# Two transformer layers on one core: the first block's V product cut finer, its weights loaded in quarters, and its k products and attention moved later

## The chip, the cores and the metric

The kernel runs on one core of a Trainium2 chip. The metric is the device time of one execution in microseconds (us), lower being better. Most executions of one kernel agree within about 0.1%, which here is 1 to 2 us. In the profiles, PE is TensorE, DVE is VectorE, ACT is ScalarE and POOL is GpSimd.

## The reference

The input x has 2048 rows of 1024 numbers in bfloat16. An attention layer A and a gated layer B are applied, and then both once more with the same weights:

```python
def A(x):                        # on layernorm(x); H = 32 heads of 32, W = 8 keys, every 2nd position back
    q, k, v = split_heads(x @ wqkv)
    kg, vg  = k[idx], v[idx]     # idx = pos - {0, 2, ..., 14}, masked below 0
    attn    = softmax(einsum("bhsd,bhswd->bhsw", q, kg) * scale)
    return merge_heads(einsum("bhsw,bhswd->bhsd", attn, vg)) @ wo

def B(x):                        # on layernorm(x); F = 3584
    gate = x @ W_gate
    return ((gate * (gate > 0)) * (x @ W_up)) @ W_down

x = x + A(layernorm(x)); x = x + B(layernorm(x))
x = x + A(layernorm(x)); x = x + B(layernorm(x))
```

## The kernel before

The rows are handled in four blocks of 512, each of four tiles of 128 rows. TensorE does all products. VectorE does the attention of a block (products of q and k, sums, weighted sums of v) while TensorE is busy with other products, and between its attention steps it multiplies gate and up (`hT`). The program is a list of steps with planned times; the steps are emitted in the order of these times, and each engine runs its own in that order. `GRP` (1.73 us) is the planned time of one group of eight 512-column products. DMA transfers are mostly issued by the sync engine (SP), one after another in the order of the program.

At the start of the program nothing can be multiplied until the first tile is loaded, normalised and turned (transposed), and the first V weights are there. Before the change, V starts on two tiles, and its weights come in two loads of 1 MB (a slab is one such load), each with all of the contraction for half of the columns:

```python
    load_x(0)                                    # the four tiles of block 0, then the weights
    ...
    def want_v(key, mid, end):                   # two slabs of 512 columns, 1 MB each
        for g in range(2):
            want((key, g), wqkv_v[:, :, 2 * D + g * SLAB:2 * D + (g + 1) * SLAB], mid if g == 0 else end)
    ...
        scratch(14)                              # ln_first: 14 products that only keep TensorE busy
        bn(0, 0); bn(0, 1); aggr(0)              # (statements joined here)
        bn(1, 0); bn(1, 1); aggr(1)
        st1 = act_stats(2)
        apply(0); turn(0); apply(1)
        copy(0, "a", 1); copy(0, "a", 0)
        turn(1)
        act_vpe(2, st1)
        copy(1, "v", 0); copy(1, "a", 1)
        bn(3, 0); bn(3, 1); apply(2); aggr(3); apply(3)
        hold["later"] = {2: (lambda: (turn(2), ...)), 4: (lambda: (turn(3), ...))}
    ...
    def v_first(ln):                             # tiles 0-1, then 2-3, then all four at once
        plan = [(c, 0, 2) for c in range(6)] + [(c, 2, 4) for c in range(6)] + [(c, 0, 4) for c in range(6, KC)]
```

The order of q and k of block 0, and the place of its attention, which the change also moves:

```python
    QK_FIRST = [(nm, c) for c in range(KC) for nm in ("q", "k")]     # q0 k0 q1 k1 ...
    QK_ORDER = [("q", 0), ("q", 1)]                                  # q0 q1, then q2 k0 q3 k1 ...
    ...
        order = QK_FIRST if n < NB else QK_ORDER
    ...
    spread(prod_sum_steps(0), t_qk0 + 3.5, 4.4)
    ev.append((t_v2 + 3.2 * GRP, lambda: head_mm(0)))                # the head sum, L
    spread(softmax_steps(0), t_v2 + 3.3 * GRP, 0.01)
    t_pv0 = t_v2 + 2.2 * GRP + 10.0
```

And the gate and up products with their accumulators. A pool of six PSUM banks serves these accumulators:

```python
    psum = ctx.enter_context(tc.tile_pool(name="psum", bufs=6, space=bass.MemoryType.PSUM))
    ...
                for nm in ("g", "u"):                                # pair j of 28
                    acc = psum.tile([P, BLK], F32, tag="acc", name=f"acc_{nm}")
                    ... # eight products into acc
                    if nm == "g":
                        ... nc.scalar.activation(rs[j][:], acc[:], ACT.Relu)      # frees the gate bank early
                    else:
                        ups[j] = acc
        def gate(j):                                                 # frees the up bank, when VectorE gets to it
                dv(nc.vector.tensor_tensor, hold["hT"][:, j, :], ups.pop(j)[:], rs.pop(j)[:], op=ALU.mult)
```

## Time and profile before

| | before |
|---|---|
| time, median of 3 runs | 1619.39 us (1618.84 to 1619.86) |
| span of the profiled execution | 1617.51 us |
| scratch products end, tile 0 turned from | 6.70, 7.36 us |
| first V product, first q product | 9.83, 24.67 us |
| first V weights landed (two loads) | 9.79, 12.79 us |
| head sum of block 0's attention | 100.74 us |

The page's first part (busy time, share of the span, instructions, per engine) and the first line of its chain of work that ended last say that the kernel is bound by TensorE (PE) from end to end:

```profile
PE 1608.1 (99%) x7505; PEld 784.1 (48%) x7554; DVE 1138.3 (70%) x963; ACT 475.8 (29%) x971; POOL 176.1 (11%) x164
...
PE 99%; DMA 0%; issue 0%; SPq 0%; DVE 0%; DVEq 0%
```

The view of waits of PE (engine, line, for what: us in total, times, longest) has four entries, all within the first 10 us:

```profile
PE scratch L132 <- DVE ones L290: 1.5, 1, 1.5
PE acc_v L132 <- DMA w_v<-in_A_wqkv_dram: 0.9, 1, 0.9
PE tp L358 <- DVE xn_first L106: 0.7, 1, 0.7
PE tp L358 <- DVE mean L106: 0.4, 1, 0.4
```

PE's timeline there (start and duration in us, then what was done, and in brackets the idle time before it with what ended it) shows where a change can gain:

```profile
6.11 0.59 PE L132 MATMUL scratch<-ones 128*128 128x512 bf16 x2
7.36 0.62 PE L358 MATMUL tp<-ident,xn_first 128*128 128x128 bf16 x8 [0.66 <-DVE xn_first L106]
8.35 0.62 PE L358 MATMUL tp<-ident,xn_first 128*128 128x128 bf16 x8 [0.37 <-DVE mean L106]
9.83 1.38 PE L132 MATMUL acc_v<-xnT_first,w_v 128*128 128x256 bf16 x11 [0.86 <-DMA w_v<-in_A_wqkv_dram]
```

Two tiles are turned before the first product, and the last thing that the first product waits for is its weights. After this PE has nothing to wait for: a microsecond gained here is worth a microsecond at the end, unless something later takes it back.

A second place: the gate and up stage of block 0, near 230 us. The timeline of all engines there (SPq is the sync engine's issue of a DMA):

```profile
228.89 1.88 DVE L106 TENSOR_TENSOR hT<-acc_u,r 128x512 bf16<-128x512 f32 x3
229.00 0.34 SPq L121 DMA_DIRECT2D s_d<-s  x1
229.07 1.89 PE L132 MATMUL acc_g<-xnT_b,w_g 128*128 128x512 bf16 x8
230.80 1.46 PE L132 MATMUL acc_u<-xnT_b,w_u 128*128 128x512 bf16 x6
```

VectorE has fallen behind and does three `hT` products in a row; the first of these, for pair 8, ends at 229.57. The up product of pair 11 starts at 230.80.

### The profile page before, as it was taken

Reading aid. Unit: us, or ns where it says so; the run is one execution under the profiler, and the core shown is the slowest. Engines: PE = TensorE matmul, PEld = TensorE weight load, DVE = VectorE, ACT = ScalarE, POOL = GpSimd, SP = SyncE. Lnnn points to the kernel's source line nnn. Section 1 sums busy time; section 2 is a strip of 40 time slices with the busy share of each in tenths; the row PEclk is TensorE's granted clock in tenths of the full one; section 3 lists DMA queues with packets and bytes.
Section 4 is the critical chain, followed back from the end, with each engine's and each line's share of the span. In section 5 each row is a group of like instructions: output and inputs, shape, how many; then the busy total and the mean of one; then the engine's idle time right before and its main releaser. Section 6 shows DMA issues by size and latency. Waiting matters only on the chain.

```text
span 1617.5 us, 18722 instructions
## 1 busy us (share of the span) xinstructions
PE 1608.1 (99%) x7505; PEld 784.1 (48%) x7554; DVE 1138.3 (70%) x963; ACT 475.8 (29%) x971; POOL 176.1 (11%) x164
## 2 busy tenths in 40 slices
PE   9999999999999999999999999999999999999999
PEld 6646544444444445444454444544445444444444
DVE  6999979996989698929489293893939939311211
ACT  4853311131116313603136031361313311131110
POOL 2300100010003002300053000530005100000000
PEclk9999999999999999999999999999999999999999
DMA  9868867697669767794747948479574884755452
GB/s 295 184 197 251 213 173 244 182 213 206 209 189 216 202 183 216 188 248 144 229 160 202 240 152 230 153 203 254 160 231 155 207 240 156 209 171 167 155 169 66
DMA packets 408440, 317.92 MB, mean 197 GB/s; under 512 B 166432, under 2 KB 389024, under 8 KB 407840
## 3 DMA queue, kind: packets, MB, share of 16 engines
q1 hardware_dynamic: 407776, 316.13, 69.4%
q8 instruction: 59, 0.97, 0.2%
q10 hardware_dynamic: 576, 0.59, 0.1%
q14 instruction: 29, 0.24, 0.1%
HBM read 266.29 MB, written 34.66 MB: 186 GB/s over the span
## 4 chain that ended last, share of the span: by engine, by line
PE 99%; DMA 0%; issue 0%; SPq 0%; DVE 0%; DVEq 0%
PE acc_u L132 24%; PE acc_g L132 24%; PE dacc L132 18%; PE acc_v L132 7%; PE acc_q L132 7%; PE acc_k L132 7%; PE acc_wo L132 7%; PE dacc_pair L132 6%; DMA w_v<-in_A_wqkv_dram 0%; PE tp L358 0%; SPq L121 0%; PE L L132 0%; DVE x L778 0%; SPq L118 0%; DVEq L1017 0%
## 5 line engine op out<-in xcount | busy, mean ns | idle before, releaser
L132 PE MATMUL acc_g<-xnT_b,w_g 128*128 128x512 bf16 x1792 | 423.3, 379 | 0.0
L132 PE MATMUL acc_u<-xnT_b,w_u 128*128 128x512 bf16 x1792 | 423.3, 379 | 0.0
L731 ACT ACTIVATE r<-acc_g 128x512 bf16<-128x512 f32 x224 | 133.6, 596 | 728.7 <-PE acc_g L132 703.8
L106 DVE TENSOR_TENSOR hT<-acc_u,r 128x512 bf16<-128x512 f32 x224 | 151.0, 687 | 243.3 <-PE acc_u L132 240.8
L132 PE MATMUL dacc<-w_d,hT 128*128 128x512 bf16 (+1 forms) x1372 | 300.4, 375 | 1.5
L132 PEld LDWEIGHTS <-hT 128*128 128x128 bf16 x1820 | 178.1, 98 | 209.0
L132 PEld LDWEIGHTS <-w_g 128*128 128x128 bf16 x1792 | 175.4, 98 | 211.4
L132 PEld LDWEIGHTS <-w_u 128*128 128x128 bf16 x1792 | 175.3, 98 | 211.4
L106 DVE TENSOR_TENSOR pv<-a,vhm 128x4096 bf16<-128x4096 bf16 x64 | 143.6, 2285 | 0.0
L778 DVE TENSOR_TENSOR x<-dacc,x 128x512 bf16<-128x512 f32 (+1 forms) x38 | 24.5, 673 | 154.1 <-PE dacc L132 154.1
L549 DVE TENSOR_TENSOR t<-q,k 128x2048 f32<-128x2048 bf16 x56 | 128.0, 2292 | 6.7 <-ACT k L485 4.6
L106 DVE TENSOR_TENSOR t<-q,k 128x2048 f32<-128x2048 bf16 x56 | 127.5, 2287 | 3.9 <-ACT k L485 2.4
L106 DVE TENSOR_TENSOR pv<-pv 128x1024 bf16<-128x1024 bf16 (+1 forms) x128 | 113.8, 952 | 0.0
L132 PE MATMUL acc_wo<-w_o,oT 128*128 128x512 bf16 x498 | 111.1, 379 | 0.7
L249 POOL TENSOR_TENSOR st_b<-st_b,neg_half 128x1 f32<-128x1 f32 x29 | 43.8, 1517 | 609.9 <-ACT st_b L248 609.9
L562 DVE TENSOR_TENSOR ac<-ac,t 128x2048 f32<-128x2048 f32 x48 | 109.7, 2285 | 0.3
L106 DVE TENSOR_TENSOR ac<-ac,t 128x2048 f32<-128x2048 f32 x48 | 109.7, 2285 | 0.0
L490 POOL COPY kh<-k 128x14 bf16<-128x14 bf16 x40 | 53.7, 1348 | 506.5 <-ACT k L485 410.4
L132 PE MATMUL dacc_pair<-w_d,hT 128*128 128x512 bf16 x413 | 95.5, 379 | 0.4
L132 PEld LDWEIGHTS <-oT 128*128 128x128 bf16 x512 | 50.1, 98 | 60.4
L244 ACT ACTIVATE xn_b<-x 128x1024 bf16<-128x1024 bf16 x29 | 30.3, 1047 | 128.6 <-DVE x L106 66.5
L410 ACT CAST vT<-acc_v 128x512 bf16<-128x512 f32 x56 | 32.7, 586 | 54.0 <-PE acc_v L132 54.0
(131 smaller groups left out, 1226.8 us busy)
## 6 DMA issues: line engine op xcount, KB each, us to landing
w_g<-in_B_W_gate_dram SPq DMA_DIRECT2D x56, 1024.0 KB, 7.2
w_u<-in_B_W_up_dram SPq DMA_DIRECT2D x56, 1024.0 KB, 5.5
w_d<-in_B_W_down_dram SPq DMA_DIRECT2D x48, 1024.0 KB, 6.0
w_o<-in_A_wo_dram SPq DMA_DIRECT2D x16, 1024.0 KB, 6.6
vhm<-v_d SPq DMA_DIRECT2D x32, 284.0 KB, 6.7
v_d<-vT SPq DMA_DIRECT2D x8, 1024.0 KB, 9.0
oT<-o_d SPq DMA_DIRECT2D x32, 256.0 KB, 4.5
w_d<-in_B_W_down_dram SPq DMA_DIRECT2D x16, 512.0 KB, 3.7
```

The source lines that it names most:

```text
L106: tail_dve[0] = f(*args, **kwargs).ins
L132: tail_pe[0] = nc.tensor.matmul(*args, **kwargs).ins
L244: nc.scalar.activation(xn, xt[:], ACT.Square, accum_out=sq)
L249: nc.gpsimd.tensor_tensor(rstd, vpe, neg_half[:, 0:1], op=ALU.pow)
L410: tail_act[0] = nc.scalar.copy(st["vT"][:, c, :], acc[:]).ins
L490: nc.gpsimd.tensor_copy(khalo[n][:, c, :], k[:, BLK:BLK + HALO])
L549: nc.vector.tensor_tensor(t[:], i0, i1, op=ALU.mult)
L562: nc.vector.tensor_tensor(o, ac[:], t[:], op=ALU.add)
L731: tail_act[0] = nc.scalar.activation(rs[j][:], acc[:], ACT.Relu).ins
L778: run = dv if n < NB - 2 else (lambda f, *args, **kwargs: f(*args, **kwargs))
```

## The change

The intent is to let PE begin V as soon as one tile is turned and a quarter of V's weights is in. V's weights are cut by the contraction instead of by columns, and each half comes in two transfers of 512 KB. V is first computed for tile 0 alone, over the first half of the contraction; tile 1, 2 and 3 follow as they become ready, and the second half is added later. The turns of tiles 1, 2 and 3 stand between V products (before, only those of tiles 2 and 3 did). A few small steps move from VectorE to ScalarE and GpSimd (POOL), x's fourth tile is loaded after the first weights, and the k products of block 0 start two PE groups later, with its attention.

```diff
-    load_x(0)
+    load_x(0, range(TPB - 1))
...
+    def want_v_first(end0, end1):
+        for hh, end in enumerate((end0, end1)):
+            want(("v0", hh), qkv_half(2, hh), end)
...
+    def load_slab(key, src):
...
+        if key[0] == "v0":
+            for i in range(2):
+                rows = slice(i * (KC // 4), (i + 1) * (KC // 4))
+                sp_dma(tv[:, rows, :], src[:, rows, :])
...
+    load_slab(("v0", 0), qkv_half(2, 0))
+    load_x(0, [TPB - 1])
+    load_slab(("v0", 1), qkv_half(2, 1))
+    load_slab(("qk01", "q", 0), qkv_half(0, 0))
...
-        scratch(14)
+        scratch(13)
         bn(0, 0); bn(0, 1); aggr(0)
+        act_square(2); act_mean(2)
         bn(1, 0)
+        apply(0, 0); apply(0, 1)
+        turn(0)
+        copy(0, "a", 0)
         bn(1, 1); aggr(1)
+        copy(0, "v", 1)
+        act_power(2)
+        apply(1, 0); apply(1, 1)
+        def second():
+            turn(1)
+            apply(2)
+            copy(1, "v", 0); copy(1, "v", 1)
+            act_square(3); act_mean(3); act_power(3)
+            apply(3)
...
-        plan = [(c, 0, 2) for c in range(6)] + [(c, 2, 4) for c in range(6)] + [(c, 0, 4) for c in range(6, KC)]
+        def head():                              # tile 0, first half of the contraction
+            for kc in range(KC // 2):
+                if kc == KC // 2 - 1:
+                    ln["second"]()
+                for c in range(KC):
+                    prod(kc, c, 0, 1)
+        ...                                      # then tiles 1, 2, 3; then the second half, two tiles at a time
...
-        order = QK_FIRST if n < NB else QK_ORDER
+        order = QK_STAGED if staged else QK_ORDER          # QK_STAGED is QK_FIRST renamed; block 0 is not staged
...
-    spread(prod_sum_steps(0), t_qk0 + 3.5, 4.4)
+    spread(prod_sum_steps(0), t_qk0 + GRP * K_STEP[0] + 1.8, 4.4)
-    ev.append((t_v2 + 3.2 * GRP, lambda: head_mm(0)))
-    spread(softmax_steps(0), t_v2 + 3.3 * GRP, 0.01)
-    t_pv0 = t_v2 + 2.2 * GRP + 10.0
+    ev.append((t_v2 + 5.2 * GRP, lambda: head_mm(0)))
+    spread(softmax_steps(0), t_v2 + 5.3 * GRP, 0.01)
+    t_pv0 = t_v2 + 4.2 * GRP + 10.0
```

Statements are joined with semicolons here, and removed helper lines are left out.

More of the change, by code (lines that the diff above doesn't have):

```diff
@@ L169, with load_x @@
         x_tiles.append(xt)
-    def load_x(b):
-        for t in range(b * TPB, (b + 1) * TPB):
+    def load_x(b, tiles=range(TPB)):
+        for t in (b * TPB + i for i in tiles):
             if t == 0:
@@ L192, in want_v, with qkv_half @@
             want((key, g), wqkv_v[:, :, 2 * D + g * SLAB:2 * D + (g + 1) * SLAB], mid if g == 0 else end)
+    def qkv_half(i, hh):
+        return wqkv_v[:, hh * (KC // 2):(hh + 1) * (KC // 2), i * D:(i + 1) * D]
+    def want_v_first(end0, end1):
+        for hh, end in enumerate((end0, end1)):
+            want(("v0", hh), qkv_half(2, hh), end)
     def want_qk(key, q_end, k_end):
@@ L196, in want_qk @@
             for hh in range(2):
-                want((key, nm, hh), wqkv_v[:, hh * (KC // 2):(hh + 1) * (KC // 2), i * D:(i + 1) * D], end)
+                want((key, nm, hh), qkv_half(i, hh), end)
     def want_wo(n, mid, end):
@@ L213, in want_down @@
             want(("d", n, half, s), wd_v[:, rows, half * SLAB:(half + 1) * SLAB], at + gap * min(8 * (s + 1), FC))
+    def load_slab(key, src):
+        shp = list(src.shape)
+        t = wring.tile([P, 8 * SLAB], BF16, tag="slab", name="w_" + "_".join(str(k) for k in key))
+        tv = t[:, 0:shp[1] * shp[2]].rearrange("p (a b) -> p a b", b=shp[2])
+        if key[0] == "v0":
+            for i in range(2):
+                rows = slice(i * (KC // 4), (i + 1) * (KC // 4))
+                sp_dma(tv[:, rows, :], src[:, rows, :])
+        else:
+            sp_dma(tv, src)
+        slab[key] = tv
     def slab_events(events):
         for i, (key, src, _) in enumerate(slab_plan):
-            def f(key=key, src=src):
-                shp = list(src.shape)
-                t = wring.tile([P, 8 * SLAB], BF16, tag="slab", name="w_" + "_".join(str(k) for k in key))
-                tv = t[:, 0:shp[1] * shp[2]].rearrange("p (a b) -> p a b", b=shp[2])
-                sp_dma(tv, src)
-                slab[key] = tv
+            if key in slab:
+                continue
             ends = sorted(end for _, _, end in slab_plan[:i])
-            events.append((ends[i - RING] + 0.3 if i >= RING else 0.1 * i, f))
+            events.append((ends[i - RING] + 0.3 if i >= RING else 0.1 * i, lambda key=key, src=src: load_slab(key, src)))
     def ln_steps(n, which, early=False, dve=()):
@@ L313, in small @@
             return stat_pool.tile([P, 1], F32, tag="f" + name, name=name, bufs=bufs)
-        mean, vpe, rstd, bst = {}, {}, {}, {}
+        mean, rstd, bst, sq = {}, {}, {}, {}
         def bn(t, half):
@@ L324, in aggr @@
             on("v", nc.vector.bn_aggr, mv[:], bst[t][:].rearrange("p a b -> p (a b)"))
-            vpe[t], mean[t] = small("vpe1"), mv[:, 0:1]
-            on("v", nc.vector.tensor_scalar, vpe[t][:], mv[:, 1:2], EPS, None, op0=ALU.add)
-            power(t)
-        def power(t):
-            rstd[t] = small("rstd1")
-            on("g", nc.gpsimd.tensor_tensor, rstd[t][:], vpe[t][:], neg_half[:, 0:1], op=ALU.pow)
-        def act_stats(t):
-            st1 = stat_pool.tile([P, 2], F32, tag="st1", name="st1")
-            on("a", nc.scalar.activation, xna[:, t, :], x_tiles[t][:], ACT.Identity, accum_out=st1[:, 0:1])
-            on("a", nc.scalar.activation, xna[:, t, :], x_tiles[t][:], ACT.Square, accum_out=st1[:, 1:2])
-            return st1
@@ L339, in act_vpe, with power, act_square @@
-        def act_vpe(t, st1):
+            mean[t] = mv[:, 0:1]
+            power(t, mv[:, 1:2], 1.0)
+        def power(t, var, sign):
+            rstd[t], vpe = small("rstd1"), small("vpe1")
+            on("g", nc.gpsimd.tensor_scalar, vpe[:], var, sign, EPS, op0=ALU.mult, op1=ALU.add)
+            on("g", nc.gpsimd.tensor_tensor, rstd[t][:], vpe[:], neg_half[:, 0:1], op=ALU.pow)
+        def act_square(t):
+            sq[t] = small("sq1")
+            on("a", nc.scalar.activation, xna[:, t, :], x_tiles[t][:], ACT.Square, scale=float(D) ** -0.5,
+               accum_out=sq[t][:])
@@ L340, in act_vpe, with act_mean, act_power @@
+        def act_mean(t):
             mn = small("mean1")
-            on("v", nc.vector.tensor_scalar, mn[:], st1[:, 0:1], 1.0 / D, None, op0=ALU.mult)
+            on("a", nc.scalar.activation, xna[:, t, :], x_tiles[t][:], ACT.Identity, scale=1.0 / D, accum_out=mn[:])
+            mean[t] = mn[:]
+        def act_power(t):
             nvar = small("nvar1")
-            on("v", nc.vector.scalar_tensor_tensor, nvar[:], st1[:, 0:1], mn[:], st1[:, 1:2], op0=ALU.mult, op1=ALU.subtract)
-            vpe[t], mean[t] = small("vpe1"), mn[:]
@@ L345, in act_vpe, with apply @@
-            on("v", nc.vector.tensor_scalar, vpe[t][:], nvar[:], -1.0 / D, EPS, op0=ALU.mult, op1=ALU.add)
-            power(t)
-        def apply(t):
-            on("v", nc.vector.tensor_scalar, xna[:, t, :], x_tiles[t][:], mean[t], rstd[t][:],
+            on("v", nc.vector.scalar_tensor_tensor, nvar[:], mean[t], mean[t], sq[t][:], op0=ALU.mult, op1=ALU.subtract)
+            power(t, nvar[:], -1.0)
+        def apply(t, half=None):
+            cols = slice(0, D) if half is None else slice(half * SLAB, (half + 1) * SLAB)
+            on("v", nc.vector.tensor_scalar, xna[:, t, cols], x_tiles[t][:, cols], mean[t], rstd[t][:],
@@ L354, in turn @@
         def turn(t):
-            tps[t] = [psum.tile([P, KC // 2, P], BF16, tag="acc", name=f"tp{h}") for h in range(2)]
+            if t == 0:
+                tps[t] = [psum.tile([P, KC // 2, P], BF16, tag="acc", name=f"tp{h}")[:] for h in range(2)]
+            else:
+                both = psum_l.tile([P, 2, KC, P], BF16, tag="L", name="tp_pair")
+                tps[t] = [both[:, h, 0:KC // 2, :] for h in range(2)]
             for c in range(KC):
@@ L362, in copy @@
             f = nc.vector.tensor_copy if eng == "v" else nc.scalar.copy
-            on(eng, f, hold["xnT"][:, t, h * (KC // 2):(h + 1) * (KC // 2), :], tps[t][h][:])
+            on(eng, f, hold["xnT"][:, t, h * (KC // 2):(h + 1) * (KC // 2), :], tps[t][h])
         warm = small("warm")
         on("a", nc.scalar.activation, warm[:], ones[:, 0:1], ACT.Identity)
-        scratch(14)
+        scratch(13)
         bn(0, 0)
@@ L370, in ln_first @@
         aggr(0)
+        act_square(2)
+        act_mean(2)
         bn(1, 0)
+        apply(0, 0)
+        apply(0, 1)
+        turn(0)
+        copy(0, "a", 0)
         bn(1, 1)
         aggr(1)
-        st1 = act_stats(2)
-        apply(0)
-        turn(0)
-        apply(1)
-        copy(0, "a", 1)
-        copy(0, "a", 0)
-        turn(1)
-        act_vpe(2, st1)
-        copy(1, "v", 0)
-        copy(1, "a", 1)
-        bn(3, 0)
-        bn(3, 1)
-        apply(2)
-        aggr(3)
-        apply(3)
-        hold["later"] = {2: (lambda: (turn(2), copy(2, "a", 0), copy(2, "v", 1))),
-                         4: (lambda: (turn(3), copy(3, "v", 0), copy(3, "a", 1)))}
+        copy(0, "v", 1)
+        act_power(2)
+        apply(1, 0)
+        apply(1, 1)
+        def second():
+            turn(1)
+            apply(2)
+            copy(1, "v", 0)
+            copy(1, "v", 1)
+            act_square(3)
+            act_mean(3)
+            act_power(3)
+            apply(3)
+        hold["second"], hold["last"] = second, last
+        hold["later"] = {t: (lambda t=t: (turn(t), copy(t, "a", 0), copy(t, "v", 1))) for t in (2, 3)}
         return hold
@@ L416, in v_first @@
         st = att[0]
-        plan = [(c, 0, 2) for c in range(6)] + [(c, 2, 4) for c in range(6)] + [(c, 0, 4) for c in range(6, KC)]
-        def f_(i, c, t0, t1):
-            def f():
-                if i == 0:
-                    st["vT"] = big_tile([P, KC, BLK], "vT_0", True)
-                acc = psum.tile([P, BLK], F32, tag="acc", name="acc_v")
-                cols = slice(t0 * P, t1 * P)
-                with pe_group():
-                    for kc in range(KC):
-                        mm(acc[:, cols], lhsT=slab[("v0", c // 4)][:, kc, (c % 4) * P:(c % 4 + 1) * P],
-                           rhs=ln["xnT"][:, t0:t1, kc, :], start=(kc == 0), stop=(kc == KC - 1))
-                tail_act[0] = nc.scalar.copy(st["vT"][:, c, cols], acc[:, cols]).ins
-                if i in ln["later"]:
-                    ln["later"][i]()
-            return f
@@ L434, in v_first, with prod @@
-        at, out = 0.0, []
-        for i, (c, t0, t1) in enumerate(plan):
-            out.append((at, f_(i, c, t0, t1)))
-            at += GRP * (t1 - t0) / TPB
-        return out
+        pairs, opened = {}, set()
+        def prod(kc, c, t0, t1):
+            part = t0 // 2
+            if (part, c // 2) not in pairs:
+                pairs[part, c // 2] = psum.tile([P, 2, BLK // 2], F32, tag="acc", name="acc_v")
+            acc = pairs[part, c // 2][:, c % 2, (t0 % 2) * P:(t0 % 2 + t1 - t0) * P]
+            with pe_group():
+                mm(acc, lhsT=slab["v0", kc // (KC // 2)][:, kc % (KC // 2), c * P:(c + 1) * P],
+                   rhs=ln["xnT"][:, t0:t1, kc, :], start=(part, c // 2) not in opened, stop=(kc == KC - 1),
+                   skip_group_check=True)
+            opened.add((part, c // 2))
@@ new lines, in head, with first_half @@
+        def head():
+            st["vT"] = big_tile([P, KC, BLK], "vT_0", True)
+            for kc in range(KC // 2):
[3 more added lines that the diff above has]
+                    prod(kc, c, 0, 1)
+        def first_half(t):
+            def f():
+                for c in range(KC):
+                    if t == 2 and c == KC // 2:
+                        ln["later"][3]()
+                    for kc in range(KC // 2):
+                        prod(kc, c, t, t + 1)
+            return f
@@ new lines, in second_half, with f @@
+        def second_half(i, t0):
+            def f():
+                if (i, t0) == (2, 0):
+                    ln["later"][2]()
+                for c in (2 * i, 2 * i + 1):
+                    for kc in range(KC // 2, KC):
+                        prod(kc, c, t0, t0 + 2)
+                tail_act[0] = nc.scalar.copy(st["vT"][:, 2 * i:2 * i + 2, t0 * P:(t0 + 2) * P],
+                                             pairs.pop((t0 // 2, i))[:]).ins
+            return f
+        tail = [(GRP * (2 + 4 * part + 0.5 * i), second_half(i, 2 * part)) for part in range(2) for i in range(KC // 2)]
@@ L440, in store_v @@
+        return head, [(GRP, first_half(1)), (4 * GRP, first_half(2)), (5 * GRP, first_half(3))] + tail
     def store_v(n):
@@ L447 @@
     khalo = {}
-    QK_FIRST = [(nm, c) for c in range(KC) for nm in ("q", "k")]
+    QK_STAGED = [(nm, c) for c in range(KC) for nm in ("q", "k")]
     QK_ORDER = [("q", 0), ("q", 1)]
@@ L486, in f @@
                     if b == 0:
-                        nc.gpsimd.memset(k[:, 0:HALO], 0.0)
+                        with (tc.issue_after(ln["last"]["g"]) if "last" in ln else nullcontext()):
+                            nc.gpsimd.memset(k[:, 0:HALO], 0.0)
                     else:
@@ L855 @@
     t_gu0 = t_fill + GRP * (4 * KC - ahead)
-    want_v("v0", t_v0 + GRP * 5, t_qk0)
+    want_v_first(t_v0 + GRP * 6, t_qk0)
     want_qk("qk01", t_qk1 + GRP * KC, t_v1)
@@ L861 @@
     want_wo(0, t_fill, t_fill)
-    for at, f in v_first(ln_a[0]):
-        ev.append((t_v0 + at, f))
+    head, steps = v_first(ln_a[0])
+    place(steps, t_v0)
+    ev.append((0.25, head))
     ev.append((0.35, lambda: load_x(1)))
-    ev.append((t_v0 + GRP * 5 + 0.6, lambda: load_x(2)))
-    ev.append((t_v0 + GRP * 5 + 0.7, zero_v))
+    ev.append((t_v0 + GRP * 6 + 0.6, lambda: load_x(2)))
+    ev.append((t_v0 + GRP * 6 + 0.7, zero_v))
     stats, apply, turn, ln_a[1] = ln_steps(1, "a", True, range(TPB))
```

## The prediction

> **What bounds the kernel.** TensorE. The page gives PE 1608.1 us busy of a 1617.5 us span and PE 99% of the chain of waits; the view of waits has no PE wait after 25 us. Only the first 10 us can be shortened. The timeline there: 14 scratch matmuls to 6.70, tile 0 turned at 7.36, tile 1 at 8.35, first V product at 9.83 (0.86 us waiting for the DMA of the first V weights, landed 9.79), then PE full until q begins at 24.67. The stretches show DMA at 350 to 390 GB/s from 6 to 26 us.
>
> **What the change does there.** V can begin once tile 0 is turned and the first 512 KB of weights are in. Estimate: these land near 7.0 us (0.75 MB of x are in at 4.95, then the rate seen). ScalarE does its two x2 passes to 7.3, then the first copy, so V begins near 7.9, 1.9 us earlier. Against this: products 128 columns wide cost more. The Trainium skill ("TensorE: Matmul & The Clock Gate", "Wait — 56ns, not 53.3ns?") gives about 2.5 ns fixed per matmul; the trace agrees (8 transposes in 0.61 us with 219 ns for one: 56 ns apart; 256 columns: 109 ns). V becomes 128 x 55.6 + 64 x 109.2 = 14.1 us (before 13.9), with three turns (1.3 us) inside instead of two (0.9 us). PE will also wait 0.3 to 0.9 us for tile 1, where POOL's two steps per tile and apply(2) stand before its copy. Estimate: q begins near 24.0, a gain of 0.7 us (0.1 to 1.2). The last V weights (near 12.3 us) come just in time. Moving k back two groups keeps k's weights (landing 24.1 and 26.8 before) from stalling it.
>
> **What it takes back.** Block 0's attention on VectorE starts two PE groups later (k0 fourth instead of second; the head sum after six V groups instead of four): 2 x 1.728 = 3.46 us later against PE. From the head sum (101.4) to 229 us the timeline shows VectorE never waiting for PE or DMA, so the lag stays. The instruction order shows one relief: POOL now does the rstd of tile 1 (LN2 of block 0) before ScalarE's, which saves about 1.0 of a 1.68 us VectorE wait near 171. Lag left: 2.4 us. Before, the gate/up stage of block 0 had these slacks (end of a VectorE product to the start of the PE group that needs its accumulator, three pairs later): 2.73 us (hT0 200.44, acc_u 203.17), 2.49 (211.04, 213.53), 1.23 (hT8 229.57, acc_u 230.80). The last one fails: PE should wait about 1.2 us for hT there, once; later VectorE idles 2 us per pair and recovers.
>
> **Sum.** 1619.4 - 0.7 + 1.2 = 1619.9; I say 1619.8 us, 8 in 10 between 1618.3 and 1621.2. All critical terms are under 0.2% of the time: within 2% 0.994, faster by over 2% 0.003, slower by over 2% 0.003.
>
> **What would show it.** The timeline: first V product near 7.9, a PE gap near 9.5 to 11 before tile 1's products, q from 24.0. Waits: one of PE acc_u for DVE hT near 230 us, 1 to 1.5 us, and no other PE wait after 25 us. Head sum 2.4 to 3.3 us later on the clock than 100.74. PE busy time up under 1 us.
>
> **What would make it wrong.** The second half of V's weights landing late (gain gone); POOL slower than I take it (0.55 us a step); VectorE's lag absorbed or larger: without the hT wait 1618.7, without POOL's relief about 1620.9. A transposed tile or a reused accumulator earlier in the same stage (slack 0.1 us for xnT_b at 191) could be the wait instead.

## The result, and the profile after

The changed kernel took 1618.30 us (median of 6 runs, 1617.89 to 1619.05) against 1619.60 us for the kernel before (6 runs beside it, 1618.76 to 1619.86). The ratio is 0.9994, with a 95% interval of 0.9981 to 1.0006: the same, within 2%. A ratio in this document is the mean time of one kernel's fast runs over that of the other's of the same rounds, so it is not quite the ratio of the medians quoted beside it. The result is correct.

The same lines as before, from the page and PE's view of waits of the kernel after:

```profile
PE 1611.1 (100%) x7633; PEld 786.4 (49%) x7633; DVE 1137.4 (70%) x960; ACT 475.5 (29%) x967; POOL 180.9 (11%) x168
...
PE scratch L132 <- DVE ones L310: 1.5, 1, 1.5
PE acc_v L132 <- ACT xnT_first L328: 0.6, 1, 0.6
PE acc_v L132 <- DVE xnT_first L106: 0.2, 1, 0.2
```

PE's busy time cannot be compared between the two pages. Some matmul records are missing from the trace of before (7505 products recorded for 7554 weight loads; after has 7633 of both), so the rise of 3.0 us is a matter of records: three later profiles with the old V and all 7554 products (e_b_queue, e_b_rotate, e_b_korder) have 1611.0 to 1611.4 us. The starts of PE groups can be compared, and PE's timeline of the first 11 us has:

```profile
6.57 0.72 PE L383 MATMUL tp<-ident,xn_first 128*128 128x128 bf16 x8
7.89 1.51 PE L132 MATMUL acc_v<-xnT_first,w_v 128*128 128x128 bf16 x24 [0.60 <-ACT xnT_first L328]
9.23 0.61 PE L383 MATMUL tp_pair<-ident,xn_first 128*128 128x128 bf16 x8
9.68 0.61 PE L132 MATMUL acc_v<-xnT_first,w_v 128*128 128x128 bf16 x8
10.47 0.72 PE L132 MATMUL acc_v<-xnT_first,w_v 128*128 128x128 bf16 x10 [0.18 <-DVE xnT_first L106]
```

V begins at 7.89 instead of 9.83. Its whole stretch is longer, as the narrow products and the three turns cost more, and q begins at 23.71 instead of 24.67. PE has thus a lead of 0.96 us over the kernel before. The lead shrinks later, and the view of waits of PE's weight loads (PEld) says where:

```profile
PEld L132 <- DMA w_u<-in_B_W_up_dram: 0.6, 1, 0.6
PEld L132 <- DMA w_o<-in_A_wo_dram: 0.5, 1, 0.5
```

Neither entry was there before. By the starts of PE groups, PE itself lost 0.17 us at 160.9 (a slab of output weights landed at 160.89, before at 157.83) and 0.26 us at 247.5 (a slab of up weights landed at 247.49, before at 244.15). The lead is then 0.52 us up to the last product. Near 230 us, where the prediction expected PE to wait for VectorE, the timeline of all engines has:

```profile
230.01 1.89 PE L132 MATMUL acc_u<-xnT_b,w_u 128*128 128x512 bf16 x8
230.43 1.88 DVE L106 TENSOR_TENSOR hT<-acc_u,r 128x512 bf16<-128x512 f32 x3
230.54 0.34 SPq L121 DMA_DIRECT2D s_d<-s  x1
```

VectorE is indeed 1.54 us later than before on the clock, with PE 0.79 us earlier. But PE's product of pair 11 starts at 230.01, although the `hT` product of pair 8 ends only at 231.11. The two do not share a bank.

At the end, the span of after is shorter by 0.855 us (1616.656 against 1617.511): 0.515 us come from PE, and 0.34 us from the time between the last product's start and the end of the span (3.36 us against 3.70). The prediction has nothing about that second part.

### The profile page after: what moved, and what is told of

Read it like the earlier page. It is cut to its first block, busy times and chain, and to the rows that moved or that the text cites. A ratio compares the mean times of both kernels' runs of the same rounds, so it can differ in the third digit from the quotient of the medians.

```text
span 1616.7 us, 18929 instructions
## 1 busy us (share of the span) xinstructions
PE 1611.1 (100%) x7633; PEld 786.4 (49%) x7633; DVE 1137.4 (70%) x960; ACT 475.5 (29%) x967; POOL 180.9 (11%) x168
## 4 chain that ended last, share of the span: by engine, by line
PE 99%; DMA 1%; DVE 0%; POOL 0%; issue 0%; DVEq 0%
PE acc_u L132 24%; PE acc_g L132 24%; PE dacc L132 18%; PE acc_wo L132 7%; PE acc_q L132 7%; PE acc_k L132 7%; PE acc_v L132 7%; PE dacc_pair L132 6%; DMA w_u<-in_B_W_up_dram 0%; DMA x<-in_A_x_dram 0%; POOL rstd L328 0%; DVE xn_first L106 0%; DVE bst L106 0%; PE tp_pair L383 0%; DVE bst L103 0%
```

## The experiments

The theory at this point had four parts. First, V gains about 1 us, and the quarters of the weights are what makes it possible. Second, the expected wait of 1.2 us is absent because banks are handed out in the order in which they are released, not in rotation. Third, VectorE's lag does cost something by another way: transfers that wait for VectorE stand in the sync engine's queue before weight loads. Fourth, the order of q and k may have a value of its own. The rival to the second part was that VectorE had caught up before 230 us. Twelve runs followed (r_after is the changed kernel again, and r_b_korder repeats e_b_korder); all gave the right result.

| run | time, median (all runs), us | before in the same rounds | ratio (95%) |
|---|---|---|---|
| r_after | 1618.04 (1617.91 to 1618.74) | 1619.25 | 0.9993 (0.9979 to 1.0006) |
| e_queue | 1619.13 (1618.74 to 1619.56) | 1619.25 | 0.9998 (0.9986 to 1.0011) |
| e_queue_copy | 1618.66 (1618.47 to 1619.28) | 1619.25 | 0.9996 (0.9983 to 1.0009) |
| e_b_queue | 1618.88 (1618.73 to 1619.33) | 1619.25 | 0.9997 (0.9984 to 1.0011) |
| e_rotate | 1619.79 (1619.16 to 1620.08) | 1619.42 | 1.0002 (0.9987 to 1.0017) |
| e_b_rotate | 1619.43 (1619.30 to 1619.55) | 1619.42 | 1.0000 (0.9985 to 1.0015) |
| e_kfirst | 1618.48 (1617.84 to 1619.37) | 1619.42 | 0.9995 (0.9980 to 1.0010) |
| e_nosplit | 1621.52 (1619.12 to 1621.98) | 1619.42 | 1.0014 (0.9997 to 1.0031) |
| e_lag2 | 1622.92 (1621.88 to 1623.45) | 1619.32 | 1.0023 (1.0006 to 1.0040) |
| e_b_korder | 1618.69 (1618.58 to 1618.84) | 1619.32 | 0.9996 (0.9981 to 1.0011) |
| e_queue_shift | 1618.21 (1618.10 to 1619.67) | 1619.26 | 0.9996 (0.9983 to 1.0010) |
| r_b_korder | 1618.92 (1618.61 to 1619.27) | 1619.26 | 0.9998 (0.9986 to 1.0011) |

"Lead" below is by how much PE is ahead of the profile of before, by the starts of the same groups. The profile of before is one execution: q starts at 24.67 us in it, and at 24.23 to 24.98 in all five profiles of kernels with the old V, since the first weights land at different times.

### r_after: the changed kernel once more

No edit.

> The changed kernel again, for a tighter time and as the neighbour of the next two. Theory (queue): V gains 0.96 us (q starts at 23.7 instead of 24.7), and 0.2 to 0.45 us of it is lost again to two late weight loads (w_o near 161 us, w_u near 247 us). Time 0.5 to 1.2 us below before. Rival (chance): those two waits were luck of one execution; then they are absent here and TensorE keeps the whole 0.96 us.

V began at 8.09 and q at 23.79, and the lead of 0.88 us stayed to the end. PEld again waited for `w_o` (0.3 us) and `w_u` (0.2 us), but PE lost almost nothing by it. The give-back by late weights is therefore between 0 and 0.43 us, from one execution to the next. The time was 1.2 us under before.

### e_rotate and e_b_rotate: banks in a forced rotation

In block 0's gate and up stage, six accumulators are allotted once and used in turn; nothing else is changed. e_rotate does this to the changed kernel, e_b_rotate to the kernel before.

```diff
-                    acc = psum.tile([P, BLK], F32, tag="acc", name=f"acc_{nm}")
+                    if n == 0:
+                        if not rot:
+                            rot.extend(psum.tile([P, BLK], F32, tag="acc", name="acc_r") for _ in range(6))
+                        acc = rot[(2 * j + (nm == "u")) % 6]
+                    else:
+                        acc = psum.tile([P, BLK], F32, tag="acc", name=f"acc_{nm}")
```

> The changed kernel, where the gate and up products of block 0 go round six fixed PSUM banks, so that up product j+3 reuses the bank of up product j: the rule that the prediction assumed. Theory (bank rule): the lag of VectorE that was predicted is real (2.3 us) and only the rule was wrong; with the rule forced, TensorE waits 1.0 to 1.3 us for hT near 230 us, once, and the time is 0.7 to 1.0 us above the changed kernel (the wait for w_u near 247 goes). Rival (lag absorbed): VectorE catches up, no wait over 0.2 us.

> The kernel before with the same forced rule, a control. Theory: smallest slack 1.2 us (hT 229.57, up product 230.80), so no TensorE wait and the time of before within 0.3 us. Rival: the forced order costs by itself, a TensorE wait of over 0.2 us.

The view of waits of PE of e_rotate has the predicted wait, once, and the timelines of PE and VectorE show that it is at the place, and about of the size, that the prediction gave:

```profile
PE acc_r L132 <- DVE hT L106: 1.1, 1, 1.1
```

```profile
231.99 1.89 PE L132 MATMUL acc_r<-xnT_b,w_u 128*128 128x512 bf16 x8 [1.10 <-DVE hT L106]
...
231.25 1.88 DVE L106 TENSOR_TENSOR hT<-acc_r,r 128x512 bf16<-128x512 f32 x3
```

PE's lead fell by 1.34 us over the stage, 1.26 of it here by the starts of the groups (the idle time of 1.10 counts from the modelled end of the product before). e_b_rotate has no wait for `hT` at all and took the time of before. So VectorE's lag is real, the rotation alone costs nothing, and the two together cost the predicted wait. That decides against the rival: VectorE had not caught up. What spares the changed kernel is the assignment of banks. In the built program, the accumulator of up product 11 lies in the bank that gate product 9 had, which ScalarE frees soon after that product ends (its Relu ran from 223.30 to 223.90), not in the bank of up product 8, which goes to up product 12. In the kernel before the built program has the same pairs, so the slack of 1.23 us that the prediction counted there was between two products with no common bank. The lag does reach ScalarE: the `r` buffers are three, so the Relu of gate product 11 waited for the same `hT` product and ran from 231.21 to 231.80, with 3.85 us idle before it instead of 2.86. PE did not need that bank so soon.

The profiled execution of e_rotate (1620.08 us) also contains 0.8 us of a later V: the first quarter of the weights landed at 8.11 us, in after at 7.33, and PE waited 1.3 us for weights. The other three executions were not profiled; their spans are 1617.4 to 1617.6 us, against a median of 1616.3 in the eleven executions of the changed kernel, which fits the wait alone.

### e_nosplit: V's weights in two loads again

```diff
-        if key[0] == "v0":
+        if False:
             for i in range(2):
```

> The changed kernel with V's weights in two 1 MB loads instead of four quarters. Theory: the first V product waits for the whole half, near 8.75 instead of 7.89 us; the gap before tile 1 takes part of that up, q starts near 24.25 (0.5 us later); with TensorE later, w_o and w_u are no longer late, so at the end it is only 0.0 to 0.2 us behind the changed kernel. Rival (quarters worth their whole 0.85 us): q at 24.5 or later and 0.5 us or more behind at the end.

PE's timeline shows that without the quarters the early turn is worth nothing:

```profile
9.07 1.12 PE L132 MATMUL acc_v<-xnT_first,w_v 128*128 128x128 bf16 x17 [1.97 <-DMA w_v<-in_A_wqkv_dram]
```

Tile 0 was turned at 6.39, but the first MB landed at 9.03, and q began at 24.79, which is 0.12 us later than before. Against the profile of after the quarters are thus worth 1.1 us, as the rival had it. The size is rough: with quarters, q began at 23.60 to 24.52 us from profile to profile, but always earlier than here. The profiled execution took 1619.12 us; the other three took 1621.4 to 1622.0, some 2.5 us more. The record lists a granted clock of 0.999 for these three and 1.000 for the profiled one. A tenth of a per cent of the span is 1.6 us (an estimate from these two figures), so the clock is a candidate for much of that; no profile shows what these executions waited for, and it stays open.

### e_queue, e_queue_copy and e_b_queue: weight loads ahead of what waits for VectorE

The two late slabs are issued before the transfers that wait for VectorE: the second slab of output weights before the loads of `oT`, the fifth slab of up weights before the store and reload of `s`. e_queue_copy also puts tile 1's copies before apply(2), against the PE gap at 10.47. e_b_queue makes the same moves in the kernel before.

```diff
-            ev.append((at + 37.5, store_s(1, 1)))
-            ev.append((at + 40.5, load_s(1)))
+            ev.append((at + 41.81, store_s(1, 1)))
+            ev.append((at + 41.815, load_s(1)))
...
-    ev.append((t_pv0 + 8.6 * 4 + 0.1, load_o(0)))
+    ev.append((t_qk2 + GRP * 16 + 0.29, load_o(0)))
...
+            early = 0.02 if key in (('o', 0, 1), ('u', 0, 4)) else 0.0      # taken off these slabs' issue times
```

```diff
             turn(1)
-            apply(2)
             copy(1, "v", 0)
             copy(1, "v", 1)
+            apply(2)
```

> The changed kernel with two moves in the sync queue: the second w_o slab is issued before the loads of oT, and the fifth w_u slab before the store of s and its reloads. Theory (queue): the weights were late because they stood in the in-order queue behind a store that waits for VectorE, which now lags by 2.3 us; both TensorE waits vanish and the lead over before stays 0.96 us to the end, about 0.4 us below the changed kernel. Rival (bandwidth or luck): w_o or w_u still lands late and TensorE still waits 0.2 us or more; time as the changed kernel's.

> As the one before, and tile 1's copies out of PSUM stand before the application of tile 2's norm on VectorE. Theory: the 0.18 us TensorE gap at 10.3 us closes, q starts at 23.5, lead over before 1.1 us. Rival: the last V weights (landing 12.1 us) hold TensorE instead, and q starts at 23.65 or later.

> The kernel before with the same two queue moves, a control. Theory (queue): before had no late weights (w_o 3.7 us, w_u 3.9 us ahead of need), so nothing changes: within 0.3 us of before. Rival: the moves help by themselves, by 0.3 us or more.

The waits for `w_o` and `w_u` were gone, and PE kept its lead to the end: 1.00 us in e_queue, 1.04 in e_queue_copy, where the 0.18 us gap was gone too (and PEld waited 0.2 us for V weights instead). So the late loads came from the order in the sync engine's queue: in after, the store of `s` is issued when VectorE has written `s` (230.54, before 229.00), and the up weights behind it are issued at 240.38 (before 237.12).

Still e_queue was 1.1 us slower than the unmodified changed kernel of the same rounds, although PE's last product was 0.12 us earlier in the profile. In the profiled executions (1618.74 against 1618.00) the loss is all after PE's end: the last two stores of the output landed 2.2 and 2.0 us after their issue, at 1615.89 and 1616.08. In r_after they took 1.3 and 1.2 us. The view of DMA of e_queue from 1612 to 1617 us has (queues with packets, MB and share; then transfers with KB and us from the start of the issue to landing):

```profile
q14 instruction: 1, 0.01, 0.4%
...
out_dram<-x ACTq DMA_DIRECT2D x1, 64.0 KB, 2.6
out_dram<-x SPq DMA_DIRECT2D x1, 64.0 KB, 2.4
```

The one packet on queue 14 is an instruction fetch of 8 KB. In e_queue it ran from 1614.70 to 1615.06, in e_queue_copy from 1614.25 to 1614.85: while the last stores were in flight. In after and r_after it started at 1615.63 and 1615.34, when the stores' data had been moved.

The packets show how the fetch and the stores met. In e_queue no packet starts between 1614.93 and 1615.04, while the fetch runs, and the view of DMA from 1614.95 to 1617 us has all that was left:

```profile
q1 hardware_dynamic: 9, 0.00, 1.0%
q10 hardware_dynamic: 9, 0.00, 0.8%
```

Each of the last two stores is 144 packets, one on queue 1 (SP) and one on queue 10 (ACT), so nine is a sixteenth: the part of one of the 16 DMA engines. These 18 packets start one after another from 1615.05, as the fetch ends, and are done at 1615.54. In e_queue_copy such a rest of 18 packets starts at 1614.85, again as the fetch ends, and is done at 1615.24. In r_after all packets of the stores were done at 1614.95.

e_b_queue showed something else. Its profile has a wait that the profile of before does not have:

```profile
27.64 1.08 PE L132 MATMUL acc_k<-xnT_first,w_qk_k 128*128 128x512 bf16 x4 [0.35 <-DMA w_qk_k<-in_A_wqkv_dram]
```

The second half of k's weights landed at 27.59 us there (26.83 in before), so with the old order of q and k, k is at the edge of a wait.

### e_queue_shift: the instruction fetch moved away

On top of e_queue, twelve stores of finished output tiles, before the last block, are each cut in four. This adds 36 transfers to the sync engine's program and leaves the last stores as they are.

```diff
-                sp_dma(out_dram[t * P:(t + 1) * P, :], x_tiles[t][:])
+                for c in range(0, D, D // 4):
+                    sp_dma(out_dram[t * P:(t + 1) * P, c:c + D // 4], x_tiles[t][:, c:c + D // 4])
```

> The kernel with the two early slab issues (e_queue), and the twelve stores of finished output tiles that come before the last block are each cut in four, which puts 36 more transfers on the sync engine some 25 to 300 us before the end and touches nothing else. In e_queue the last instruction fetch (8 KB) ran at 1614.70 to 1615.06 us, among the last output stores, and these landed 2.0 us after issue instead of 1.3. Theory 1 (that fetch delays the last stores, and it is the sync engine's): the fetch moves out of the last 5 us, the last store lands 1.2 to 1.4 us after issue, tail 3.3 to 3.5 us, time 1617.9 to 1618.3, that is 0.7 to 1.0 us under e_queue. Theory 2 (the fetch belongs to another engine, or the slow landing has another cause): the fetch is still in the last 5 us; if it lies within the stores again, the tail stays near 4.2 and the time near 1619.1.

The fetch was gone from the end (the last one on queue 14 is at 1495.1 us), and the last stores landed in time. The same view of DMA of e_queue_shift has no line for queue 14, and:

```profile
out_dram<-x ACTq DMA_DIRECT2D x1, 64.0 KB, 1.7
out_dram<-x SPq DMA_DIRECT2D x1, 64.0 KB, 1.6
```

The time was 1618.21 us, 0.9 under e_queue, though e_queue was measured beside another set of runs of before (1619.25 there, 1619.26 here). From the start of the last product to the end of the span it is 3.48 us, against 4.20 in e_queue. So the fetch belongs to the sync engine, and, with the packets above, it was what delayed the stores. The lines of all fourteen profiles agree: the fetch comes at a fixed place in the sync engine's program, so the number of recorded sync instructions decides where it falls.

| recorded sync instructions | profiles | fetch starts, after the last store's issue ended, us | last store landed, after its issue ended, us |
|---|---|---|---|
| 853 | before, e_b_rotate | 2.32, 2.33 | 1.27, 1.28 |
| 854 | e_nosplit, e_b_korder, r_b_korder | 2.04 to 2.06 | 1.24 to 1.28 |
| 855 to 857 | after, r_after, e_kfirst, e_b_queue, e_rotate, e_lag2 | 1.12 to 1.25 | 1.23 to 1.28 |
| 859 | e_queue, e_queue_copy | 0.64, 0.22 | 2.02, 1.77 |
| 899 | e_queue_shift | far earlier | 1.28 |

The span also ends 1.27 and 1.28 us after the last landing in the two profiles with 853, and 0.90 to 1.10 us in all others (1.04 in e_queue_shift, with no fetch there). In those two, the fetch runs at the very end (1617.28 to 1617.59 in before, which ends at 1617.51). The 0.34 us that the changed kernel gained at its end thus go with three more sync instructions, which moved the fetch. That this part is caused by the fetch is argued from the table and was not tested alone.

For the mechanism, the Trainium skill ("DMA: Bandwidth & Descriptors", Queues, rings and completion order) says that a DMA engine takes turns between the queues that have work for it, and that the write that signals completion lands only after every earlier write of that engine, across its queues. That fits stores that are delayed by a fetch on another queue; the runs show the delay, 0.5 to 0.8 us, and a sixteenth of each store that moved only when the fetch had ended; what the completing write itself waited for they do not show.

### e_kfirst, e_b_korder and r_b_korder: the order of q and k

e_kfirst undoes the order of q and k and the later attention in the changed kernel. e_b_korder does only this part in the kernel before; r_b_korder is the same kernel again.

```diff
-        order = QK_FIRST if n < NB else QK_ORDER
+        order = QK_FIRST if staged else QK_ORDER
...
-    spread(prod_sum_steps(0), t_qk0 + 3.5, 4.4)
+    spread(prod_sum_steps(0), t_qk0 + GRP * K_STEP[0] + 1.8, 4.4)
...                                        # head_mm, softmax and t_pv0 two GRP later, as in the change
```

The edit of e_kfirst is the reverse of this, in the changed kernel.

> The changed kernel with block 0's q and k products alternating again and attention placed as before. Theory (k order needed): k0 reaches its second half of weights at 26.3 us, these land near 27.0; TensorE waits 0.5 to 0.9 us for w_qk_k, and the lead over before falls from 0.96 to 0.1 to 0.45 us; no later waits for w_o or w_u. Rival (k order idle): no wait, lead 0.96 us kept to the end, which makes it faster than the changed kernel by 0.4 us.

> The kernel before with only the k order and the later attention of the change (V as before). Theory: VectorE lags by 2.3 to 2.5 us in the gate stage, but TensorE is not early, so w_o and w_u come just in time: no TensorE wait over 0.1 us, time within 0.3 us of before. Rival (lag costs by itself): a wait of 0.3 us or more for w_o, w_u or hT, and that much more time.

> The kernel before with only the new order of q and k and its later attention, once more, for the size of its part and for a second profile. Theory 1 (the order alone is worth something, since in the old order the k groups sometimes wait for k's weights): 0.4 to 0.8 us under the kernel before, ratio 0.9995 to 0.9998, no PE wait for the k weights. Theory 2 (the 0.63 us of the first look were chance): within 0.2 us of the kernel before.

The one profile of e_kfirst has no wait for k's weights (they landed at 23.18 and 25.94, earlier than in any other profile), and PE's lead of 1.07 us stays to the end. Its four runs fall in two groups, 1617.84 and 1617.96, and 1619.00 and 1619.37. A wait for k's weights in some executions would do that, but only the fast kind was profiled, so it is not shown.

e_b_korder was 0.63 us under before, r_b_korder 0.34. Their profiles do not credit this to the order. In both, PE's lead is there at the first V product (0.44 and 0.24 us), where the order of q and k cannot act yet, and stays the same to the end; it comes from V weights that landed earlier. Another 0.2 us is the end after the last landing (1.06 and 1.07 us against 1.27), which goes with one more sync instruction. A wait for k's weights was seen in one of the four profiles with the old order (before, e_b_rotate, e_kfirst and e_b_queue, the last of which has it) and in none of those with the new order. The own value of the order is therefore somewhere between nothing and the few tenths that such a wait costs now and then; these runs do not settle it.

### e_lag2: the attention two more groups later

The head sum and what follows it is put another two groups later, to see how much lag the program bears. (A first build failed, as the steps of block 1's sums no longer came in a possible order; their spacing was cut from 4.5 to 3.0.)

```diff
-    ev.append((t_v2 + 5.2 * GRP, lambda: head_mm(0)))
-    spread(softmax_steps(0), t_v2 + 5.3 * GRP, 0.01)
-    t_pv0 = t_v2 + 4.2 * GRP + 10.0
+    ev.append((t_v2 + 7.2 * GRP, lambda: head_mm(0)))
+    spread(softmax_steps(0), t_v2 + 7.3 * GRP, 0.01)
+    t_pv0 = t_v2 + 6.2 * GRP + 10.0
...
-    spread(sums1[:4], t_pv0 + 34.5, 4.5)
+    spread(sums1[:4], t_pv0 + 34.5, 3.0)
```

> The changed kernel with block 0's head sum two V groups later still (3.46 us more lag of VectorE). Theory (queue): the second w_o slab stands behind loads that wait for VectorE, lands near 164.3 instead of 160.9, and TensorE waits 3.2 to 3.7 us for the DMA of w_o; no wait for VectorE itself over 0.3 us; time 3.0 to 3.6 us above the changed kernel. Rival (PSUM): TensorE waits about 3 us for VectorE's additions to x, near 170 us. Rival (slack): no wait, time unchanged.

After 25 us PE waited twice, and both in the stage of the output product, earlier than the place that the prediction had picked:

```profile
163.37 8.81 PE L132 MATMUL acc_wo<-w_o,oT 128*128 128x512 bf16 x40 [1.85 <-DMA w_o<-in_A_wo_dram]
173.38 1.89 PE L132 MATMUL acc_wo<-w_o,oT 128*128 128x512 bf16 x8 [1.21 <-DVE x L106]
```

By the starts of the groups PE lost 3.4 us. The head sum came 4.0 us later than in after (107.27 against 103.23), but 0.6 us of this were there when q began (24.30 against 23.71), so nearly all of the added lag was lost. The first wait is again a weight load behind transfers that wait for VectorE; the second is VectorE itself, which frees the accumulators of the output product. So the lag of the change just fits into the program's slack, and twice as much does not. The profiled execution took 3.5 us more than that of after, as expected; the other three took 0.8 to 1.6 us more still, and as in e_nosplit the record lists a clock of 0.999 for them.

## Why the prediction was right or wrong

The predicted time, 1619.8 us in a range of 1618.3 to 1621.2, holds the measured 1618.3 only at its lower edge; that is luck more than merit, since the sum contains a wait of 1.2 us that did not come. The class, the same within 2%, was right, and could hardly fail with all terms under 0.2%. Point by point:

- **What bounds the kernel** was right. PE was full before and after, and of its work only the first 10 us could be shortened.
- **V's start** was right: 7.9 predicted, 7.89 measured, and the last thing that the first V product waited for was ScalarE's copy, as stated.
- **V's gain** had the right mechanism. Predicted were 0.7 us (0.1 to 1.2); the first pair of profiles has 0.96. Over all profiles q starts at a mean of 24.57 us with the old V (five profiles) and 23.92 with the new one (seven, without e_nosplit and e_queue_copy), which is 0.65 us, so the 0.96 holds some chance. One term was of the wrong size: the PE gap for tile 1 was put at 0.3 to 0.9 us, and it was 0.18 us in the first profile and nothing in the second. POOL's two steps, which the gap was to come from, took 0.19 and 0.55 us.
- **The cost of narrow products** was right in kind. The estimate, which took the fixed 2.5 ns per matmul from the Trainium skill ("TensorE: Matmul & The Clock Gate", "Wait — 56ns, not 53.3ns?"), gives 14.1 us of V and 1.3 of turns, 15.4 in all. Without a gap it measured 15.70 us (8.09 to 23.79 in r_after); 0.3 us of it are not accounted for.
- **VectorE's lag** was right: the head sum was predicted 2.4 to 3.3 us later than 100.74 and came 2.49 later. The relief by POOL was right in kind as well: VectorE's waits for `rstd` from 101 to 229 us fell from 2.3 to 1.4 us in the view of waits. Against PE, the lag near 230 us was 2.3 us (1.54 on the clock and 0.79 of PE's lead); 2.4 was predicted.
- **The wait for `hT`** was the step that failed. The prediction counted an accumulator as needed again "three pairs later" and concluded "The last one fails: PE should wait about 1.2 us for hT there, once". The wait was absent. The prediction had named this case among those that would make it wrong, "without the hT wait 1618.7", but for another reason, that the lag would be absorbed. e_rotate, which forces the assumed rule, has the wait at the predicted place with 1.10 us of idle time. So under that rule the slack, the lag and the place were right; the assumption that six banks are used in rotation was wrong. The changed kernel takes the bank of a gate product, released early.
- **"No other PE wait after 25 us"** was wrong in a small way. PEld waited for two weight loads, and PE lost 0.43 us by it in one profile and almost nothing in the other. The lag does reach PE, by the sync engine's queue rather than by a bank; e_queue shows it by taking it away.
- **PE's busy time**, "up under 1 us", was right: 1611.0 to 1611.4 us with the old V where all records are there, and 1611.1 in after.
- **Not foreseen:** the end of the kernel, 0.34 us shorter.

Put together for the profiled execution: the wait that did not come, -1.2; V's larger gain, -0.26; late weights, +0.43; the end, -0.34. That is 1.37 us under the 1619.9 of the prediction's sum, or 1618.5. The profiled execution took 1618.37 us; the rest lies outside the profiled span. No version tried beats the changed kernel beyond the spread of the runs: e_queue_shift, with both repairs, took 1618.21 us, against 1618.04 and 1618.30 for the changed kernel itself.

## What to carry to other kernels

When you argue that an engine will wait for a buffer, read from the built program which buffer it really gets: a pool that hands out the first bank released hides a lag that a rotation would expose. When one engine falls behind, look at what stands behind its transfers in an in-order issuing queue, because weight loads that have nothing to do with it come late. When effects of a tenth of a per cent are weighed, compare the starts of the same groups in two profiles and the end after the last product separately, since a few added DMA instructions can move an instruction fetch into the last stores and hide or fake a gain of this size.

## What the Trainium skill lacked or had wrong

- "Runtime: NRT & Kernel Launch" (Instruction fetch mechanics) calls the cost of crossing a fetch boundary mostly hidden. Here, a fetch of 8 KB among the last output stores delayed the last landing from about 1.25 us after issue to 1.77 and 2.02 us, and moving it away took the time from the last product's start to the end of the span from 4.20 to 3.48 us. No page says that a fetch can delay a store at the end of a kernel.
- The same section gives 16 KiB as the size of a refill. The page of before has 59 fetches with 0.97 MB on queue 8, which is 16 KB each, but 29 with 0.24 MB on queue 14, which is 8 KB each, and the sync engine's are among these.
- "Perfetto Trace Analysis" (Optimizing Tensor Performance, Matmuls) advises that independent groups rotate through the PSUM banks. Where two kinds of accumulators are freed by different engines, a strict rotation over six banks put a wait of 1.10 us before PE that handing them out in order of release did not have. The page does not mention this choice.
